# Making q, k and v of a gated attention/MLP kernel in row halves of 64 that change banks half way

## Chip, cores, metric

One Trainium2 chip; the kernel runs on 1 of its cores. The metric is the device time of one execution in microseconds. Five engines work beside each other, each through its own queue in order: TensorE (PE; its weight loads are listed apart as PEld), VectorE (DVE), ScalarE (ACT), GpSimd (POOL) and SyncE (SP), which issues the DMAs here.

## What is computed

```python
S, D, H, F = 2048, 576, 32, 4608          # Dh = 18, all float32
g = sigmoid((x * gate_w).sum(-1, keepdims=True))
q, k, v = split(x @ wqkv)                  # 3 x 32 heads of 18
a = softmax(q @ k.T * Dh ** -0.5) @ v      # per head
a = a.reshape(S, D) @ wo
y = layernorm(x)
b = gelu(y @ w1 + b1) @ w2 + b2
out = g * a + (1 - g) * b
```

## The kernel before

The work is recorded in the order in which the Python code emits it: there is no scheduler, each engine runs its instructions as written, and waits are put between them where a tile is written or read.

**Products.** Every float32 operand is split in a rounded high part and the rest (`hi`, `lo`), and a product is the sum of three: hi·hi, hi·lo, lo·hi. D = 576 is four chunks of 128 and one of 64. The last chunk's high and low part lie in one tile of 128 rows (`big[0:64, 8]`, `big[64:128, 8]`), with the weights of that chunk twice below each other. So an accumulation is 4 x 3 + 2 = 14 matmuls of 128 rows.

**The first stage** (L712 to L1022, some 216 us) makes q, k and v. x is worked on in four blocks (`tb`) of 512 tokens. Per block there are 17 groups in a list `work`: nine `qk_group` (128 output columns of wqkv, all 512 tokens: 14 matmuls of 512 columns into one PSUM bank) and eight `v_group` (128 tokens, half of v's 576 columns: 14 matmuls of 288 columns). A qk group is then copied out by ACT (`hh`, L896), its rest is made by DVE (`hl`, L897), and both go to DRAM (`qk_scr`). A v group is copied by ACT (first half, L918 and L920) or DVE (second half, L922).

After each group g the loop emits what hangs on it, "the hook of g" below:
- `x_chunk(tb + 1, c)`, in five consecutive hooks: chunk c of the next block of x is transposed by PE (four 128x128 transposes into a bank, L766). DVE subtracts the mean for the MLP (L781), ACT rounds the high part (L783), DVE makes the low part (L784); in the trace ACT starts when L781 has ended. In block 0 `y_chunk` does the like for the block's own normed rows.
- `norm`, `stat_rows`, `load_wide`: the layer norm's statistics on DVE, their transpose, and a broadcast load of mean and 1/std that L781 needs.
- `next_round`, twice in the hooks that the table `ROUNDS` names: a round of the attention's first pass, two matmuls of 54 rows (rows 0 to 53 and 64 to 117, L229) into two banks, each reduced to its maximum by DVE (L231). Forty rounds in twenty hooks lie in this stage: three hooks of block 1, nine of block 2, eight of block 3.
- loads of q, k and weights, and pieces of the MLP's preparation.

**Banks.** The stage uses eight PSUM banks: four (`ps_a`) go round among groups and transposes, and four (`ps_s1` with three, `ps_o` with one; `score_bank` goes round them) that belong to the rounds.

**After it** follow attention and MLP together: a step of scores, exponentials and P·V with pieces of the MLP between. Matmuls there are pairs of 64 rows (or 54, 56): one on rows 0 to 63 and one on rows 64 to 127, into two banks. `out_pair` (L548) exchanges them half way: in its first half (`turn` 0) rows 0 to 63 add to bank 0 and rows 64 to 127 to bank 1, in its second the other way round, so that both banks get the whole sum. So that no bank gets both at once, PE waits between the turns on a semaphore `swap` (L567), which ACT raises (`sem_inc`, L585) when both last matmuls of the first turn have ended.

## Time and profile before

| what | us |
|---|---|
| median of 3 runs | 2225.52 (2225.38 to 2226.88) |
| profiled execution, first to last instruction | 2224.1 |
| first stage: PE's last v matmul ends, first score matmul starts | 216.3 |
| its block 0, q and k; then v | to 40.1; to 60.7 |
| its blocks 1, 2, 3 | to 110.35, 165.36, 216.27 |
| ACT, POOL busy in the whole span | 1428.9, 1003.0 |

The span and the median differ by 1.4 us, which lie around the program. Times of the stage's parts are starts of instructions in the timeline. A row of the timeline merges instructions of one line: start, time from the first start to the last end, engine, line, operation, shapes (rows*columns of the weights, then output), count. As a matmul's end overlaps the next one's start, the pitch of a stream is read from starts, not from durations. The granted TensorE clock is 1.000 throughout.

### The profile page before, as it was taken

What the parts mean: (1) busy time and instruction counts of PE and PEld (TensorE: products, weight loads), DVE (VectorE), ACT (ScalarE), POOL (GpSimd) and SP (SyncE); (2) the same over time, 40 slices, a digit from 0 to 9 for tenths busy, and PEclk for the clock granted to TensorE, in tenths of its full rate; (3) what the DMA queues carried; (4) which work ended last, traced back from release to release, by engine and by line L of the source; (5) the groups of instructions that cost most, each with busy time, mean ns of one, the idle gap of its engine ahead of it and who ended that gap; (6) DMA issues with size and microseconds to landing.
All of it is one profiled execution on the core that took longest, in us unless ns stands there. A gap on an engine that the chain in (4) does not pass through costs nothing.

```text
span 2224.1 us, 51508 instructions
## 1 busy us (share of the span) xinstructions
PE 2206.3 (99%) x20528; PEld 1576.1 (71%) x20528; DVE 1642.5 (74%) x2856; ACT 1428.9 (64%) x2655; POOL 1003.0 (45%) x1001
## 2 busy tenths in 40 slices
PE   8999999999999999999999999999999999999999
PEld 7878666766667766777766776776776776776668
DVE  6685777777778778777777777777777777777734
ACT  4333777777776666666666666666665666666772
POOL 4331766666664444444444444444444444444710
PEclk9999999999999999999999999999999999999999
DMA  8767555444464623333354424232464323242264
GB/s 266 268 222 223 192 174 162 147 159 148 153 197 136 195 101 121 123 120 104 114 171 149 137 79 137 100 124 100 120 178 146 107 102 123 101 150 92 89 223 168
DMA packets 164119, 329.23 MB, mean 148 GB/s; under 512 B 56830, under 2 KB 84090, under 8 KB 153150
## 3 DMA queue, kind: packets, MB, share of 16 engines
q1 hardware_dynamic: 161782, 322.19, 44.7%
q8 instruction: 162, 2.65, 0.5%
q10 hardware_dynamic: 1968, 3.70, 0.5%
q14 instruction: 79, 0.65, 0.1%
q0 software_dynamic: 128, 0.03, 0.0%
HBM read 233.47 MB, written 96.17 MB: 148 GB/s over the span
## 4 chain that ended last, share of the span: by engine, by line
PE 91%; DVE 3%; DMA 2%; ACT 2%; issue 1%; POOL 1%; SPq 0%; DVEq 0%; ACTq 0%; POOLq 0%
PE ps L288 20%; PE ps L578 20%; PE ps L490 20%; PE ps L270 13%; PE ps L229 11%; PE ps L890 3%; PE ps L1225 3%; PE ps L911 1%; DVE m L231 1%; DMA p<-in_A_wqkv_dram 1%; ACT zz L543 1%; DMA x<-in_B_w_dram 1%; POOL w L182 0%; PE ps L766 0%; ACT p L273 0%
## 5 line engine op out<-in xcount | busy, mean ns | idle before, releaser
L231 DVE TENSOR_REDUCE m<-ps 128x1 f32<-128x512 f32 x2048 | 1311.8, 685 | 408.9 <-PE ps L229 397.6
L273 ACT ACTIVATE p<-ps 128x512 f32<-128x512 f32 x1048 | 566.8, 596 | 264.4 <-PE ps L270 260.8
L273 ACT ACTIVATE ring<-ps 128x512 f32<-128x512 f32 x1000 | 542.3, 596 | 291.6 <-PE ps L270 288.9
L490 PE MATMUL ps<-big,w 64*128 64x512 f32 x3708 | 567.1, 392 | 0.2 <-issue 0.2
L182 POOL TENSOR_SCALAR zz<-zz 128x512 f32<-128x512 f32 x288 | 178.3, 619 | 744.4 <-ACT zz L543 712.1
L578 PE MATMUL ps<-w,hh 64*128 64x288 f32 x4352 | 484.0, 294 | 1.0 <-DVE x L595 0.9
L270 PE MATMUL ps<-qa,ka 56*128 56x512 f32 x2048 | 457.1, 420 | 3.2 <-ACT p L273 1.7
L578 PEld LDWEIGHTS ps<-w,hh 64*128 64x128 f32 x4352 | 423.0, 186 | 28.8 <-DVE x L595 3.6
L229 PE MATMUL ps<-ka,qa 54*128 54x512 f32 x2048 | 433.1, 398 | 0.6
L490 PEld LDWEIGHTS ps<-big,w 64*128 64x128 f32 x3708 | 365.8, 186 | 71.4 <-issue 0.5
L182 POOL TENSOR_TENSOR zz<-zz,z 128x512 f32<-128x512 f32 x288 | 371.5, 1290 | 24.0
L270 PEld LDWEIGHTS ps<-qa,ka 56*128 56x128 f32 x2048 | 210.5, 184 | 210.6 <-DVE m L231 165.0
L578 PE MATMUL ps<-w,hl 64*128 64x288 f32 x2176 | 347.4, 292 | 0.8 <-POOL hl L182 0.8
L288 PE MATMUL ps<-p,vt 128*32 128x512 f32 x1968 | 239.2, 598 | 0.0
L229 PEld LDWEIGHTS ps<-ka,qa 54*128 54x128 f32 x2048 | 217.1, 184 | 25.3 <-DVE m L231 5.2
L578 PEld LDWEIGHTS ps<-w,hl 64*128 64x128 f32 x2176 | 230.1, 185 | 1.2 <-POOL hl L182 1.1
L288 PE MATMUL ps<-ring,vt 128*32 128x512 f32 x1872 | 227.6, 598 | 0.0
L182 POOL TENSOR_TENSOR hl<-zz,hh 128x512 fp32r<-128x512 f32 x136 | 175.1, 1287 | 11.3
L182 POOL TENSOR_TENSOR w<-x,w 128x576 fp32r<-128x576 f32 (+1 forms) x54 | 99.5, 1858 | 167.4 <-ACT w L394 141.2
L288 PEld LDWEIGHTS ps<-p,vt 128*32 128x32 f32 x1968 | 52.5, 109 | 112.1 <-issue 102.7
L288 PEld LDWEIGHTS ps<-ring,vt 128*32 128x32 f32 x1872 | 49.9, 109 | 106.5 <-issue 106.5
L595 DVE SCALAR_TENSOR_TENSOR x<-ps,x 128x288 f32<-128x288 f32 x256 | 104.1, 449 | 8.7 <-PE ps L578 8.4
(123 smaller groups left out, 1549.8 us busy)
## 6 DMA issues: line engine op xcount, KB each, us to landing
w<-w_scr SPq DMA_DIRECT2D x54, 1152.0 KB
w<-w_scr SPq DMA_DIRECT2D x108, 576.0 KB
x<-in_B_w_dram SPq DMA_DIRECT2D x72, 288.0 KB
w_scr<-w SPq DMA_DIRECT2D x18, 1152.0 KB
w_scr<-w SPq DMA_DIRECT2D x36, 576.0 KB
qa<-qk_scr SPq DMA_DIRECT2D x192, 72.0 KB
ka<-qk_scr SPq DMA_DIRECT2D x84, 144.0 KB
qk_scr<-hh SPq DMA_DIRECT2D x36, 256.0 KB
```

Of the source, the lines that this page charges most:

```text
L182: fn(*args, **kw)
L229: nc.tensor.matmul(ps, qa[r0:r0 + 54, t * P:(t + 1) * P], ka[r0:r0 + 54, kb * TB:(kb + 1) * TB], start=True, stop=True)
L231: nc.vector.tensor_reduce(M4[u][:, h, t, kb:kb + 1], ps, axis=AX.X, op=ALU.max)
L270: nc.tensor.matmul(ps[h], ka[r0:r0 + 56, kc * P:(kc + 1) * P], qa[r0:r0 + 56, qb * TB:(qb + 1) * TB], start=True, stop=True)
L273: nc.scalar.activation(p_of(n)[:, qb, h], ps[h], AF.Exp, scale=SCALE)
L288: nc.tensor.matmul(OB[u][r:r + 32, :], v[:, k, 19 * h:19 * h + 32], p_of(c)[:, qb, h, :], start=(k == 0), stop=(k == NT - 1))
L490: nc.tensor.matmul(ps[h], wt[w_][r, c, :], y[r, c, :], start=(k == 0), stop=(k == 26))
L543: defer(2, lambda w=w, z=z: nc.scalar.activation(w, z, AF.Square))
L578: mm = nc.tensor.matmul(ps[nn][:, :ND], h_[r, tok], w_[p_][r, cs[nn]], start=(k == 0), stop=(k == 6 * G - 1))
L595: nc.vector.scalar_tensor_tensor(dst, ps[nn][:, :ND], 0.5, b2b[:, cs[nn]] if g == 0 else dst, op0=ALU.mult, op1=ALU.add)
L890: nc.tensor.matmul(ps, w_[:, c, ms], big[:, s_, :], start=(k == 0), stop=False)
L1225: nc.tensor.matmul(ps[:, :ND], OT[b][2][:, s_, tok], w_part(w_, c)[:, cs], start=(k == 0), stop=(k == 13))
```

## The change

From block 0's v on there are no groups. A *unit* (`half_unit`) makes two output tiles at once, in two banks of `ps_a`: two qk tiles, both halves of v for 128 tokens, or the tile 4 alone in two halves of 256 tokens. It runs as pairs of 64-row matmuls in two turns, 14 pairs and 13, with the exchange of banks and the `swap` semaphore between. Units go two by two through the stage: first turn of A, first turn of B, second turn of A, second turn of B. Blocks are not kept apart: v's last unit of a block goes with q/k's first of the next. Hooks stand after each turn (after the second only, for tile 4), again 17 a block, and their tables are moved by one place here and there.

Transposes become pairs of 64 rows, into two banks of `score_bank` rather than one of `ps_a`; what reads them works on 256 columns, twice. The last chunk's missing row halves are kept in `X4`, which lies in K's second buffer `KA[1]`; two rows of ones are copied back there at step 5 of the attention. Block 0's q and k, with the transposes before them, stay as they were.

```diff
-        def transposed(tb, c):
-            ps = psum(ps_a)
-            for t in range(4):
-                nc.tensor.transpose(ps[:, t * P:(t + 1) * P], x_view(tb)[:, t, c * P:(c + 1) * P], ident)
-            return ps
+        def turned_over(src, rows=P):
+            banks = [score_bank() for _ in range(2)]
+            for t, part in enumerate(src):
+                for h in range(2):
+                    r = slice(64 * h, 64 * h + 64)
+                    nc.tensor.transpose(banks[h][:rows, 64 * t:64 * t + 64], part[r], ident[r, r])
+            return banks
...
             if tb > 0:
-                nc.vector.tensor_tensor(y, ps, wide[:, 0, :], op=ALU.subtract)
+                for ps, of in pieces:
+                    nc.vector.tensor_tensor(of(y), ps, of(wide[:, 0, :]), op=ALU.subtract)
             if c < 4:
-                nc.scalar.activation(big[:, c, :], ps, AF.Copy)
-                nc.vector.tensor_tensor(big[:, 4 + c, :], ps, big[:, c, :].bitcast(F32), op=ALU.subtract)
+                for ps, of in pieces:
+                    nc.scalar.activation(of(big[:, c, :]), ps, AF.Copy)
+                    nc.vector.tensor_tensor(of(big[:, 4 + c, :]), ps, of(big[:, c, :]).bitcast(F32), op=ALU.subtract)
...
+        def half_unit(unit, turn):
+            kind, tb, a, b = unit["of"]
+            if turn == 0:
+                unit["ps"] = [psum(ps_a) for _ in range(2)]
             else:
+                nc.tensor.wait_ge(swap, unit["turned"])
+            ps = unit["ps"]
+            terms = [(c, k) for c in range(4) for k in range(3)] + ([(4, 1)] if turn else [(4, 0), (4, 2)])
+            for i, (c, k) in enumerate(terms):
+                ends = []
+                for h in range(2):
+                    o = h ^ turn
+                    r = slice(64 * h, 64 * h + 64)
+                    w_ = (W_V if kind == "v" else W_QK)[k // 2][r, c, :]
+                    xs = x_rows(tb, k % 2, c, h)
...
+                    ends.append(nc.tensor.matmul(out_, left, right, start=(turn == 0 and i == 0), stop=(turn == 1 and i == 12)))
+            if turn == 0:
+                unit["turned"] = exchange(ends)
+                return
...
+        units = [("v", 0, t, None) for t in range(4)]
+        for tb in range(1, NB):
+            units += [("qk", tb, 4, None)] + [("qk", tb, fst, snd) for fst, snd in ((0, 1), (2, 3), (5, 6), (7, 8))]
+            units += [("v", tb, t, None) for t in range(4)]
...
+        for i in range(0, len(units), 2):
+            for half in range(2):
+                for unit_ in units[i:i + 2]:
+                    kind, tb, _, snd = unit_["of"]
+                    half_unit(unit_, half)
+                    if kind == "v" or snd is not None or half == 1:
...
+                        hooked(tb, nth[tb])
+                        nth[tb] += 1
```

`exchange` is the `sem_inc` of `out_pair` as a function: one ACT instruction that waits for both matmuls in `ends`.

PE in block 2, from the end of a qk group or turn over the hook that holds a chunk of x and two rounds (hook 7; `ps` is a bank, `big` x's transposed parts, `wqk` weights, `ka_108` the `X4` parts). Before:

```order
L892 MATMUL ps<-big,wqk_126 128x512
L893 MATMUL ps<-big,wqk_127 128x512
L766 MATMUL ps<-ident,x 128x128 [waits DVE_49]
L766 MATMUL ps<-ident,x 128x128 x3
L229 MATMUL ps<-ka_107,qa_104 128x512 [waits DVE_49] x4
L890 MATMUL ps<-big,wqk_126 128x512 [waits DVE_49]
```

The same place in the change:

```order
L956 MATMUL ps<-ka_108,wqk_126 128x512
L956 MATMUL ps<-big,wqk_126 128x512
L773 MATMUL ps<-ident,x 128x64 [waits DVE_49] x2
L773 MATMUL ps<-ident,x 128x64 x6
L229 MATMUL ps<-ka_107,qa_104 128x512 [waits DVE_49,PE_49] x4
L956 MATMUL ps<-big,wqk_126 128x512 [waits swap]
```

All six instructions work in halves of 64 rows now, and the rounds' four matmuls (L229) wait for banks that the chunks of x have just used: the transposes and the rounds go round the same four.

DVE at the same place, hooks 6 to 9 of block 2 (`hl` are q/k's low parts, `p` and `big` what is made of a chunk of x, `m` the maxima of the rounds). Before:

```order
L897 TENSOR_TENSOR hl<-ps,hh 128x512
L781 TENSOR_TENSOR p<-ps,qa_106 128x512
L784 TENSOR_TENSOR big<-ps,big 128x512
L897 TENSOR_TENSOR hl<-ps,hh 128x512
L781 TENSOR_TENSOR p<-ps,qa_106 128x512
L784 TENSOR_TENSOR big<-ps,big 128x512
L231 TENSOR_REDUCE m_1041<-ps 128x1 x4
```

In the change:

```order
L801 TENSOR_TENSOR p<-ps,qa_106 128x4x64 x2
L805 TENSOR_TENSOR big<-ps,big 128x4x64 x2
L970 TENSOR_TENSOR hl<-ps,hh 128x512 x2
L801 TENSOR_TENSOR p<-ps,qa_106 128x4x64 x2
L805 TENSOR_TENSOR big<-ps,big 128x4x64 x2
L231 TENSOR_REDUCE m_1405<-ps 128x1 x4
```

The low parts of a unit come two at a time, ahead of the hook's chunk, and the chunk's own work is in pieces of 256 columns.

PE at the start of block 0's v (`wv_128` and `wv_129` are the high and low parts of v's weights). Before:

```order
L892 MATMUL ps<-big,wqk_126 128x512
L893 MATMUL ps<-big,wqk_127 128x512
L911 MATMUL ps<-wv_128,big 128x288 [waits DVE_49,Activation_49]
L911 MATMUL ps<-wv_129,big 128x288 [waits Pool_49]
L911 MATMUL ps<-wv_128,big 128x288 x2
```

In the change:

```order
L914 MATMUL ps<-big,wqk_127 128x512
L956 MATMUL ps<-wv_128,big 128x288 [waits DVE_49,Activation_49] x2
L956 MATMUL ps<-wv_128,big 128x288 x2
L956 MATMUL ps<-wv_129,big 128x288 [waits Pool_49]
L956 MATMUL ps<-wv_129,big 128x288 [waits DVE_49]
```

The third pair needs the low weights of both halves of v, the first made by POOL and the second by DVE; before, the second half's were first read 14 matmuls later.

## Prediction

> **What bounds the kernel now.** First the page: span, busy times, the chain that ended last.

> ```profile
> span 2224.1 us, 51508 instructions
> ...
> PE 2206.3 (99%) x20528; PEld 1576.1 (71%) x20528; DVE 1642.5 (74%) x2856; ACT 1428.9 (64%) x2655; POOL 1003.0 (45%) x1001
> ...
> PE 91%; DVE 3%; DMA 2%; ACT 2%; issue 1%; POOL 1%; SPq 0%; DVEq 0%; ACTq 0%; POOLq 0%
> ```

> PE is busy for 99% and is 91% of the chain, so what PE saves in the first stage moves the end, unless another engine then holds it. Attention keeps its order. Next, the stage in windows (block 0's v, blocks 1, 2, 3; columns PE, PEld, DVE, ACT, POOL):

> ```profile
> 40.00:61.00 21.00, 20.25 (x155) 19.59 (x154) 16.13 (x28) 7.63 (x18) 6.42 (x5) 1.00 0.71 238
> 61.00:110.00 49.00, 48.27 (x269) 41.60 (x269) 32.48 (x69) 14.86 (x33) 13.48 (x11) 1.00 0.81 269
> 110.00:165.00 55.00, 54.89 (x299) 43.82 (x295) 44.24 (x89) 19.78 (x39) 18.55 (x15) 1.00 0.65 225
> 165.00:216.00 51.00, 51.00 (x275) 40.71 (x273) 30.80 (x56) 16.60 (x28) 11.04 (x6) 1.00 0.70 224
> ```

> PE is full in all four. DVE comes next: 44.2 of 55 us in block 2, 16.1 of 21 in block 0. Whatever PE saves, DVE must keep up with.

> **Part 1: one matmul in 28 goes.** The timeline gives pitches, from start to start: full groups first, then 64-row pairs in attention.

> ```profile
> 44.56 1.76 PE L911 MATMUL ps<-wv,big 128*128 128x288 f32 x12
> ...
> 46.43 0.60 PE L766 MATMUL ps<-ident,x 128*128 128x128 f32 x4
> ...
> 67.21 2.91 PE L890 MATMUL ps<-big,wqk 128*128 128x512 f32 x12
> ...
> 70.41 2.91 PE L890 MATMUL ps<-big,wqk 128*128 128x512 f32 x12
> ...
> 698.50 0.96 PE L578 MATMUL ps<-w,w 64*128 64x288 f32 x12
> 699.29 0.41 PE L229 MATMUL ps<-ka,qa 54*128 54x512 f32 x2
> ...
> 776.24 1.10 PE L490 MATMUL ps<-big,w 64*128 64x512 f32 x8
> 777.16 0.41 PE L229 MATMUL ps<-ka,qa 54*128 54x512 f32 x2
> 777.40 1.10 PE L490 MATMUL ps<-big,w 64*128 64x512 f32 x8
> ```

> A v group takes 46.43 - 44.56 = 1.87, 0.133 a matmul of 14; a 64-row pair of 288 columns (699.29 - 698.50) / 6 = 0.132. A qk group takes 70.41 - 67.21 = 3.20, 0.229 a matmul; a pair of 512 columns (777.40 - 776.24) / 5 = 0.232. So a pair costs what a full matmul costs, and 27 pairs replace 28 matmuls. v: 16 units save 0.13 each, 2.1. q and k: 12 units fall from 6.40 to 27 x 0.232 = 6.26, 1.7 in all; tile 4's pairs have 256 columns, which no row shows: between half of 0.232 and 0.132 I take 0.118, 27 of them 3.19 against 3.20, nothing. **Saved: 3.8** (between -1 and +1 of that for tile 4).

> **Part 2: PE no longer changes between 128 and 64 rows.** Twenty hooks have rounds of 54 rows between full groups. One of them:

> ```profile
> 91.49 0.29 PE L914 MATMUL ps<-wv,big 128*128 128x288 f32 x1
> 91.71 0.74 PE L229 MATMUL ps<-ka,qa 54*128 54x512 f32 x4
> 92.38 1.85 PE L911 MATMUL ps<-wv,big 128*128 128x288 f32 x12
> 94.07 0.29 PE L913 MATMUL ps<-wv,big 128*128 128x288 f32 x1
> ```

> From 91.49 to 94.07 are 2.58 us for 13 v matmuls (13 x 0.132 = 1.72) and two pairs of 512 columns (0.46): 0.40 too much. In attention no such excess stands between 64-row and 54-row pairs: the five pairs from 776.24 run at one pitch. **Saved: 20 x 0.40 = 8.0.**

> **Part 3: transposes.** Two chunks at once, in block 0's v:

> ```profile
> 48.71 1.03 PE L766 MATMUL ps<-ident,x 128*128 128x128 f32 x8
> 49.50 1.84 PE L911 MATMUL ps<-wv,big 128*128 128x288 f32 x12
> ```

> Eight take 0.79, 0.10 each with 128 columns loaded and 128 moving. Eight half-row ones of 64 moving columns replace four. If loads set the pitch, four pairs cost the same 0.4; if moving columns do, 0.2; if the halves don't overlap, 0.8. I take 0.4, since the loads keep their 128 columns: 20 chunks, nothing gained (-4 to +8).

> [...]

> **Part 4: the waits that go, and those that come.** Before, the 176.2 us from 40.10 to 216.27 hold 27 qk groups (86.4), 32 of v (59.8 at 1.87), 20 chunks (8.0), 40 rounds (9.3), the excess (8.0) and some 0.5 of small transposes: 172.0. So PE waits **4.2** in all, and these waits I replace by new ones.

> *The start of v.* The timeline there:

> ```profile
> 40.10 1.76 PE L911 MATMUL ps<-wv,big 128*128 128x288 f32 x12
> ...
> 41.03 1.65 DVE L761 TENSOR_TENSOR wv<-p,wv 128x1440 fp32r<-128x1440 f32 x1
> ...
> 42.74 1.72 PE L911 MATMUL ps<-wv,big 128*128 128x288 f32 x11 [0.47 <-DVE wv L761]
> ```

> DVE ends the second half's low weights at 42.68. The change needs them in its third pair, at 40.36, so PE waits 2.4 until 42.74, with all of v behind it. DVE's order ahead of that instruction is unchanged. **+2.4.**

> *Banks.* Transposes and rounds share four banks now. The latencies, from timelines and from groups of the first 40 us:

> ```profile
> 63.78 0.39 PE L893 MATMUL ps<-big,wqk 128*128 128x512 f32 x1
> ...
> 64.25 0.60 ACT L896 ACTIVATE hh<-ps 128x512 fp32r<-128x512 f32 x1 [1.14 <-issue]
> ...
> 64.88 0.69 DVE L897 TENSOR_TENSOR hl<-ps,hh 128x512 fp32r<-128x512 f32 x1 [0.83 <-ACT hh L896]
> ...
> 134.51 2.48 DVE L231 TENSOR_REDUCE m<-ps 128x1 f32<-128x512 f32 x4
> ...
> L761 DVE TENSOR_TENSOR wqk<-p,wqk 128x256 fp32r<-128x256 f32 x1 | 0.4, 418 | 0.0
> L760 ACT ACTIVATE wqk<-p 128x256 fp32r<-128x256 f32 x1 | 0.4, 405 | 0.0
> ```

> Block 2, hook 7: let P be the time at which PE goes on after the turn (64.00 in these rows). ACT starts at P + 0.25, the first low part at P + 0.88. DVE's pitch is some 0.6 at 512 columns (2.48 for four) and 0.34 at 256 (0.42 less the same overlap). So the unit's two low parts take DVE to P + 2.1, and the chunk's four pieces end at P + 3.7. The hook's second round needs this chunk's two banks: PE gets there at P + 0.7 and gets them at P + 3.4 and 3.8. Wait: 3.1. Behind it in PE's queue is the whole next turn. Hook 9, by the same steps, with the rounds in both preceding chunks' banks: 2.4. Block 1, hook 10: DVE has hook 9's four reductions (2.5) ahead of the chunk, so the banks come at P + 6.6 of the turn before: 3.8. **Sum 9.3**; at the least nothing, if DVE is ahead.

> Smaller ones by the same steps: DVE's lag at the end of block 0's v 0.4, hooks 11 and 16 of block 2 1.4, five hooks of rounds in a row in block 3 1.6, ACT's pieces of the MLP ahead of v's copies at the stage's end 1.2, the last unit's banks at the MLP's first matmul 0.6: 5.2. Each hangs on a few tenths; I take half, **2.6** (0 to 5.2).

> *Semaphore.* Each exchange needs one ACT instruction:

> ```profile
> L585 ACTq EVENT_SEMAPHORE  x144: 17/17/17, 255.3 to 2134.7; - x144
> ...
>   PEld ps L578: 1.2, 6
> ```

> In attention 144 of these held PE six times, 1.2 in all. Here the other unit's turn (1.8 or 3.2) lies between. Nothing; if ACT is late, see the rivals.

> DVE's and ACT's extra pieces (256 columns twice) are in the latencies above. POOL's two memsets less and the two copies at step 5 lie beside PE's work: nothing.

> **Sum**, against the profiled span: -3.8 - 8.0 - 4.2 + 2.4 + 9.3 + 2.6 = -1.7, 2222.4; the median lies 1.4 above the span: **2224**.

> **Rivals.**
> *A, the forecast:* banks eat the gain. For it: DVE's 44.2 us in block 2, and units whose low parts come two at a time ahead of the chunk. 2224; with the smaller waits between none and all, and 3 us either way for the transposes and the large waits, 2219 to 2228.

> [...]

> *B, banks come in time:* if PE's waits shrink to the start of v and at most half of the 9.3, the sum is -13.6 to -9: 2212 to 2217. For it: before, DVE ran without a pause for long in block 2 and PE lost little. Against it: those rounds had four banks to themselves.

> *C, the semaphore, slower:* `sem_inc` stands in ACT's queue behind copies that wait for DVE. When ACT is later than the other unit's turn, 1.8 in v, PE waits at the exchange. If most of v's 16 exchanges lose 0.5 on top of A, that is 8: 2232.

> *D, no single mode:* if half-row transposes of 64 columns or the exchange cost a drain like the rounds did, 8.0 comes back: 2232.

> **How the numbers follow.** A 0.47, B 0.28, C 0.20, D 0.05. A measurement tells 0.2% from no change, 4.5 us: faster is below 2221.1. That is B and a fifth of A: 0.38. Same: the rest of A but its top, 0.36. Slower: C, D and that top, 0.26. The range leaves out B's best cases and the worse half of C and D: 2213 to 2231. A's own is 2219 to 2228.

> **What would show it.** Part 1 and 2: pitches of 0.13 and 0.23 for the unit's pairs, and no excess around L229 in the stage. Part 3: the pitch of the L773 pairs, 0.1. Part 4: PE idle 2.4 at 40.4 for v's weights; gaps of 2 to 4 us ahead of L229 in hook 10 of block 1 and hooks 7 and 9 of block 2, ended by DVE's pieces of a chunk; the stage ending at 213 to 217 instead of 216.3. Waits put down to ACT at the exchange would speak for C. The prediction is wrong if the half-row transposes cost twice, or if DVE's pieces of 256 columns are far from 0.42.

## The result, and the profile after

The changed kernel takes **2244.45 us** (median of 5, 2242.23 to 2246.21) against 2225.52 (median of 5, 2225.22 to 2226.88): ratio 1.0082, 95% interval 1.0071 to 1.0093. It is slower by 18.9 us, where 2224 was forecast with 2231 as the upper end. The profiled execution took 2242.23 us, the shortest of the five; its span is 16.3 us longer than that of before, and it is these 16.3 that the trace can explain. From the page of the changed kernel:

```profile
span 2240.4 us, 53493 instructions
...
PE 2203.1 (98%) x21459; PEld 1583.4 (71%) x21459; DVE 1647.1 (74%) x2901; ACT 1431.7 (64%) x2684; POOL 999.7 (45%) x999
...
PE 87%; DVE 3%; POOL 2%; ACT 1%; issue 1%; DMA 0%; SPq 0%; DVEq 0%; POOLq 0%; ACTq 0%
```

PE is busy for 3 us less in a span that is 16 us longer. The windows show where (changed kernel, the columns of before: PE, PEld, DVE, ACT, POOL busy, then the granted clock):

```profile
40.00:61.00 21.00, 17.65 (x277) 16.69 (x278) 15.86 (x39) 7.79 (x24) 5.94 (x5) 1.00 0.62 208
61.00:110.00 49.00, 43.46 (x449) 37.51 (x447) 30.26 (x75) 12.15 (x32) 9.92 (x8) 0.93 0.75 241
110.00:165.00 55.00, 49.03 (x535) 45.35 (x531) 41.48 (x99) 17.44 (x45) 18.21 (x15) 0.97 0.68 211
165.00:216.00 51.00, 49.38 (x525) 43.10 (x525) 31.50 (x60) 16.86 (x31) 7.55 (x6) 1.00 0.81 241
```

PE was full in all four; now it idles 3.4, 5.5, 6.0 and 1.6 us of them, and in two the clock is no longer 1.00. The view of PE's waits in the stage, before first, then after (us in total, times, longest; only named releasers):

```profile
PE ps L766 <- DVE big L784: 0.7, 1, 0.7
PE ps L911 <- DVE wv L761: 0.5, 1, 0.5
PE ps L911 <- DVE big L784: 0.3, 1, 0.3
```

```profile
PE ps L229 <- DVE big L805: 8.1, 4, 3.7
PE ps L229 <- ACT oe L246: 1.8, 1, 1.8
PE ps L956 <- DVE wv L763: 1.7, 1, 1.7
PE ps L229 <- DVE ka L811: 1.3, 2, 0.8
...
PE ps L229 <- ACT strow L857: 1.0, 1, 1.0
```

Over nine of these microseconds stand ahead of a score round (L229) and end with DVE's pieces of an x chunk (L805, L811): the banks that transposes and rounds share.

**An account of the stage**, from the first matmul of v to the first L270. *Work* is each matmul at the pitch of its kind (the pitches of the prediction; 0.09 for a pair of transposes); *waits* are the times from one start to the next above that pitch, where they exceed 0.25 us (they come out larger than the idle times of the views, because a matmul's end overlaps the next one's start: 0.39 long at a pitch of 0.23 with 512 columns); *clock* is what matmuls took longer in stretches granted 0.5; *small* is the rest, in which the mode changes of before lie (0.40 a hook of rounds in the prediction's rows). The last column goes from the first L270 to the last P·V matmul (L288 in both kernels).

| kernel | stage | work | small | waits | clock | time behind, against before |
|---|---|---|---|---|---|---|
| before | 176.2 | 163.7 | 8.4 | 4.0 | 0 | 0 |
| changed | 189.3 | 158.5 | 0.9 | 26.3 | 3.6 | +3.3 |
| e_share | 187.8 | 163.7 | 7.5 | 10.2 | 6.3 | +0.4 |
| e_full | 198.1 | 159.3 | 7.5 | 25.5 | 5.8 | +2.0 |
| e_rounds | 184.4 | 158.5 | 0.3 | 20.9 | 4.7 | +7.0 |
| e_b3 | 175.8 | 158.5 | 0.5 | 16.7 | 0 | +7.1 |
| e_c4 | 170.2 | 158.5 | 0.5 | 11.1 | 0 | +1.4 |

The gain came in full: 5.2 of work and 7.5 of mode changes. Against it stand 22.3 more of waits and 3.6 of clock: 13.1 net. The other 3.3 us are lost in attention, whose order did not change. The 7.0 and 7.1 of e_rounds and e_b3 hold the same losses, with 6.8 us at half clock behind the wait near 520 (and 3.4 more near 2141 in e_rounds); e_share loses another 0.8 behind its last P·V matmul.

### The profile page after: what moved, and what is told of

The parts are those of the page before. It is cut to its first block, busy times and chain, and to the rows that moved or that the text cites. A ratio compares the mean times of both kernels' runs of the same rounds, so it can differ in the third digit from the quotient of the medians.

```text
span 2240.4 us, 53493 instructions
## 1 busy us (share of the span) xinstructions
PE 2203.1 (98%) x21459; PEld 1583.4 (71%) x21459; DVE 1647.1 (74%) x2901; ACT 1431.7 (64%) x2684; POOL 999.7 (45%) x999
## 4 chain that ended last, share of the span: by engine, by line
PE 87%; DVE 3%; POOL 2%; ACT 1%; issue 1%; DMA 0%; SPq 0%; DVEq 0%; POOLq 0%; ACTq 0%
PE ps L288 20%; PE ps L495 20%; PE ps L583 19%; PE ps L270 12%; PE ps L229 10%; PE ps L956 3%; PE ps L1300 3%; DVE m L231 1%; POOL zz L182 1%; ACT zz L548 1%; DMA low<-ot_scr 0%; PE ps L244 0%; ACT p L273 0%; DVE x L596 0%; POOL w L182 0%
## 5 line engine op out<-in xcount | busy, mean ns | idle before, releaser
L231 DVE TENSOR_REDUCE m<-ps 128x1 f32<-128x512 f32 x2048 | 1311.8, 684 | 412.2 <-PE ps L229 398.4
L270 PE MATMUL ps<-qa,ka 56*128 56x512 f32 x2048 | 457.1, 421 | 4.4 <-ACT p L273 1.8
L229 PE MATMUL ps<-ka,qa 54*128 54x512 f32 x2048 | 439.9, 398 | 14.6 <-DVE big L805 8.1
L270 PEld LDWEIGHTS ps<-qa,ka 56*128 56x128 f32 x2048 | 210.6, 184 | 211.9 <-DVE m L231 165.3
L229 PEld LDWEIGHTS ps<-ka,qa 54*128 54x128 f32 x2048 | 222.2, 185 | 39.5 <-issue 6.9
L288 PE MATMUL ps<-p,vt 128*32 128x512 f32 x1968 | 239.2, 598 | 0.0
L288 PE MATMUL ps<-ring,vt 128*32 128x512 f32 x1872 | 227.6, 598 | 0.0
L288 PEld LDWEIGHTS ps<-p,vt 128*32 128x32 f32 x1968 | 52.6, 109 | 112.1 <-issue 102.8
L288 PEld LDWEIGHTS ps<-ring,vt 128*32 128x32 f32 x1872 | 50.0, 109 | 106.4 <-issue 106.4
```

The source lines that it names most:

```text
L229: nc.tensor.matmul(ps, qa[r0:r0 + 54, t * P:(t + 1) * P], ka[r0:r0 + 54, kb * TB:(kb + 1) * TB], start=True, stop=True)
L231: nc.vector.tensor_reduce(M4[u][:, h, t, kb:kb + 1], ps, axis=AX.X, op=ALU.max)
L270: nc.tensor.matmul(ps[h], ka[r0:r0 + 56, kc * P:(kc + 1) * P], qa[r0:r0 + 56, qb * TB:(qb + 1) * TB], start=True, stop=True)
L288: nc.tensor.matmul(OB[u][r:r + 32, :], v[:, k, 19 * h:19 * h + 32], p_of(c)[:, qb, h, :], start=(k == 0), stop=(k == NT - 1))
```

## The experiments

Times are medians, each beside runs of the kernel before on the same chip (2225.0 to 2225.5).

**One part alone, in the kernel before: e_share.**

```
-            ps = psum(ps_a)
+            ps = psum(ps_a) if first else score_bank()
```

> The kernel before, with one part of the change alone: the transposes of x behind the first block (20 chunks) go into the four score banks, which the rounds use, instead of the groups' four. No pairs, no new order, 128 rows. If the sharing of the banks by itself makes PE wait, gaps of 1 to 3 us ahead of L229 appear in block 2 at the hooks that have a chunk and rounds (7 and 9) and in block 0's v, 6 to 12 us in all: 2231 to 2239. If the waits come from the tempo instead (a PE that has become 7% faster ahead of a DVE with no less to do), the slower order before the change has room for most of them: 3 us or less, 2226 to 2229.

Measured: 2237.5, ratio 1.0050 (1.0033 to 1.0067). From its waits, timeline (start, duration, engine, line, operation; in brackets the idle time before and what ended it) and windows:

```profile
PE ps L229 <- DVE big L784: 4.2, 3, 2.4
PE ps L229 <- DVE big L789: 2.0, 1, 2.0
```

```profile
142.66 0.69 DVE L897 TENSOR_TENSOR hl<-ps,hh 128x512 fp32r<-128x512 f32 x1 [0.64 <-ACT hh L896]
143.27 0.68 DVE L781 TENSOR_TENSOR p<-ps,qa 128x512 f32<-128x512 f32 x1
...
144.62 0.69 DVE L784 TENSOR_TENSOR big<-ps,big 128x512 fp32r<-128x512 f32 x1 [0.66 <-ACT big L783]
...
145.46 0.46 PE L229 MATMUL ps<-ka,qa 54*128 54x512 f32 x1 [2.41 <-DVE big L784]
```

```profile
142.60:146.00 3.40, 0.99 (x5) 0.35 (x4) 2.67 (x5) 0.63 (x2) 1.26 (x1) 1.00 0.42 154
146.00:149.40 3.40, 3.40 (x9) 2.63 (x10) 1.70 (x3) 0.00 (x0) 0.00 (x0) 0.50 0.02 5
```

The chain is the prediction's at hook 7: group's low part, chunk's subtraction, ACT's copy, chunk's low part, and only then the round. It makes the stage 11.6 us longer without a single pair: 6.2 of waits and 6.3 of clock, less 0.9 of small excess. At hooks 7 and 9 of block 2 the waits are 4.9, against 5.2 in the changed kernel: there the shared banks alone are enough, at the old tempo as well, and the rival of the tempo falls. In the whole stage e_share has 6.2 of new waits, the changed kernel 22.3. Block 0's v, where waits had been expected too, has none here and 2.4 behind its first waits in the changed kernel: there the tempo or the pieces of 256 columns must take part, and no run separates these.

**The banks' phase in attention: e_ring and e_ringb.** Where attention's steps begin, `ring[0] += 2` in the changed kernel, `ring[0] += 3` in the kernel before.

> The changed kernel, with the counter that picks the next score bank set on by two where attention's steps begin, so that the steps find the phase modulo 5 that they had before the change (80 banks drawn until then before, 128 after). Phase theory: the +3.8 us that the changed kernel loses behind the first L288 (one step of 2.3 to 2.5 near 520 us, 1.3 near 2140) and part of the 1.2 us that its first L270 waits for v's last copy come from that phase; then the waits near 529 and 2142 vanish and the time falls by 4 to 5 us, to about 2240. Chance theory: those stalls are transfers that land at other moments; then they stay or move, and the time stays within 1.5 us of 2244.5.

> The kernel before, with the same counter set on by three where the steps begin, so that it has the changed kernel's phase and nothing else of the change. Phase theory: stalls of 2.3 to 2.5 us near 517 us and 1.3 near 2125 appear, and up to 1.2 at the first L270: 2229 to 2231. Chance theory: 2225.5, within 1 us.

Measured: 2240.13 (2239.45 to 2241.99), 4.3 below the changed kernel; and 2228.51, ratio 1.0017 (1.0008 to 1.0027), 3.5 above the kernel before. Timelines of e_ringb, and of the changed kernel at the same step:

```profile
515.83 0.50 PE L270 MATMUL ps<-qa,ka 56*128 56x512 f32 x1 [0.67 <-DVE m L231]
...
518.29 0.79 PE L229 MATMUL ps<-ka,qa 54*128 54x512 f32 x1 [1.49 <-DVE m L231]
```

```profile
529.40 0.50 PE L270 MATMUL ps<-qa,ka 56*128 56x512 f32 x1 [0.67 <-DVE m L231]
...
531.86 0.50 PE L229 MATMUL ps<-ka,qa 54*128 54x512 f32 x1 [1.49 <-DVE m L231]
```

The same two waits, to the hundredth, come with the phase, and in e_ring's trace this step has neither. Which bank a step draws depends on how many were drawn before it, and the change draws 128 where 80 were drawn. In e_ringb the two were followed by 6.8 us at half clock, so the same step costs 2.5 us in the changed kernel's trace and 5.4 in this one. Why just this phase lets an L270 meet a bank that DVE still reads stays open.

The wait near 2140, which the same expectations put down to the phase, does not belong to it: 1.3 us in the changed kernel, it is still 1.1 in e_ring and 1.2 in e_c4, both with the phase of before, and e_ringb, with the changed one, has next to none (0.2). In the changed kernel PE waits there for DVE, and DVE for a load:

```profile
2141.38 0.69 DVE L1213 TENSOR_TENSOR x<-x,low 128x512 f32<-128x512 f32 x1 [7.84 <-DMA low<-ot_scr]
...
2142.49 0.77 PE L583 MATMUL ps<-w,hh 64*128 64x288 f32 x3 [1.36 <-DVE x L596]
```

Every run with the new stage has this wait (0.6 to 2.9), e_share does not; why the load comes later against PE's work is open. So of the 3.3 us lost in attention the phase is 2.5 and this wait 1.3; 0.6 is gained near 416.

**Rounds away from the chunks: e_rounds.** Only the two rows of the table of rounds change:

```
-lambda g: 2 * (g in (9, 10, 16)), lambda g: 2 * (g % 2 or g == 16),
+lambda g: 2 * (g in (9, 15, 16)), lambda g: 2 * (g in (2, 4, 5) or g > 10),
```

> The changed kernel with the score rounds moved off the hooks that transpose x: block 1 hooks 9, 15, 16 instead of 9, 10, 16; block 2 hooks 2, 4, 5 and 11 to 16 instead of 1, 3, 5, 7, 9, 11, 13, 15, 16. The same 40 rounds. Theory of the shared banks: the waits of 4.0 (block 1, hook 10), 3.05 and 2.2 (block 2, hooks 7 and 9) and 1.3 (hook 3) go, some tenths come at the new places; PE's busy share stays over half in every 3.4 us, so the granted clock stays 1.0 there and another 3 to 4 us come back: the stage ends 10 to 13 us earlier, 216 to 219 instead of 229.35, and the time is 2231 to 2235. Rival, DVE is behind anyway: the waits only move to the next users of the banks, and the stage ends at 226 or later.

Measured: 2238.58, stage end 224.87. It lies between the two: the named waits went, and of their 10.6 us half came back at the new places:

```profile
110.45 0.46 PE L229 MATMUL ps<-ka,qa 54*128 54x512 f32 x1 [0.81 <-DVE ka L811]
...
111.77 0.47 PE L229 MATMUL ps<-ka,qa 54*128 54x512 f32 x1 [0.86 <-DVE ka L811]
```

```profile
133.99 2.48 DVE L231 TENSOR_REDUCE m<-ps 128x1 f32<-128x512 f32 x4
...
134.74 2.29 PE L229 MATMUL ps<-ka,qa 54*128 54x512 f32 x4 [0.46 <-DVE m L231]
```

DVE has 2.5 us of reductions for a hook of two rounds and up to 1.5 more of low parts or sums, in a turn of 1.85 or 3.2: where the rounds stand close, it is late again.

**Rounds to where DVE has room: e_b3.** The same 40 rounds, most of them in block 3, one a hook in v's turns.

```
+lambda g: 2 * (g in (9, 16)), lambda g: {2: 1, 5: 1, 12: 1, 13: 1, 14: 1, 15: 1, 16: 2}.get(g, 0),
+lambda g: 2 if g < 10 or g == 16 else 1]
```

> The changed kernel with most score rounds moved into block 3, where DVE has room, one a hook in the stretches of v: block 1 hooks 9 and 16 (two each), block 2 hooks 2, 5 and 12 to 15 (one each) and 16 (two), block 3 two in each of the first ten hooks and in the last, one in the others. The same 40 rounds. Theory that PE waits because DVE has more to do in a turn than the turn is long, and holds the shared banks meanwhile: with one round or none in a turn that has a chunk, the waits in blocks 1 and 2 fall from 17 us to 5 or less and block 3 gets 1 to 3: the stage ends at 214 to 219, 2229 to 2235. Rival, the banks' count alone decides (two banks for a chunk, two for a round, whatever DVE does): waits stay near 20, and the stage ends at 225 or later.

Measured: 2231.79, stage end 216.06, no stretch at half clock in the stage. The waits in blocks 1 and 2 fell from 15 to 6. So the banks' count alone is not the bound: with two banks for a chunk and two for a round most of PE's waits there go, if DVE can empty them within the turn. In the whole stage 16.7 are left.

**PE kept busy: e_warm.** Pairs of no use between the two rounds of block 1's hook 10 (16) and block 2's hook 9 (10); what they write is written over.

> The changed kernel with matmuls of no use put between the two rounds of block 1's hook 10 (16 pairs of 64 rows and 512 columns, 3.7 us) and of block 2's hook 9 (10 pairs, 2.3 us), into banks that the next unit starts afresh, so that PE works through two of the waits. Clock theory: the wait at hook 10 makes PE idle for over half of two windows of 3.4 us, and the two windows behind run at half clock; kept busy, PE keeps 1.0, no stretch at 0.5 stays in the stage, and the 3.6 us that its matmuls lost there come back, less what the useless work overruns the waits (0.5 or so): 2240 to 2242. Rival, the clock falls for another reason, or costs nothing because DVE is late anyway: stretches of 0.5 stay, or the stage ends no earlier than 229.

Measured: 2241.43 (2239.41 to 2246.6), the profiled one 2246.6, with the stage's end at 233.31. Inconclusive: the median lies in the forecast range, but stretches at 0.5 stayed, as its rival had it. Behind the smaller waits ahead of hook 10 a stretch at 0.5 began at 99.1 already, and further ones came at 150, 167 and 222, so the cost of the clock was not isolated in this way.

**Full transposes again: e_full.**

```
-            if first:
-                ps = psum(ps_a)
+            if True:
+                ps = psum(ps_a) if first else score_bank()
```

> The changed kernel with one part undone: behind the first block, the transposes of x are again four of 128 rows into one score bank for each chunk (20 chunks), and their readers work on 512 columns at once. Theory that full rows between 64-row pairs cost a mode switch as the rounds did before the change: each chunk shows 0.2 to 0.4 us above its transposes, 4 to 8 us in all, against which one bank for each chunk instead of two and DVE pieces of 0.69 instead of twice 0.42 take 5 to 10 us from the waits of 26.3: the stage ends at 223 to 231 and the time is 2238 to 2246. Rival, the switch costs nothing with transposes and only the fuller banks count: the stage ends at 220 or earlier.

Measured: 2249.05, ratio 1.0107 (1.0092 to 1.0122). Small excess rose from 0.9 to 7.5, 0.33 for each of 20 chunks, as the mode theory has it; but the waits stayed, so the single bank for a chunk brought nothing, and that part of the expectation was wrong. In this stream of pairs half-row transposes were the right ones.

**Small things, and both together: e_small, e_best2.**

```
-6: (2, (0, 1)), 7: (3, (2,)), 8: (3, (3,))}
+7: (2, (0, 1)), 8: (3, (2, 3))}
...
-            if tb == 1 and g == 5:
+            if tb == 1 and g == 4:
                 load_q(0)
...
+                nc.vector.tensor_copy(mr, ps[:32, :P])
...
+    ring[0] += 2
```

> The changed kernel with five small things moved, each at a place of its own: the first block's last two norm steps behind the split of v's second half of weights; load_q and load_k of block 1 at hook 4 instead of 5, ahead of the store of the statistics; in block 0 x's chunk ahead of y's in each hook; the copy of the maxima's transposed rows by DVE instead of ACT in the stage; and the phase of e_ring. Theory by places: v's first waits fall from 2.8 to about 1; the wait at block 1's hook 10 falls from 4.0 to about 1.7, since the broadcast of the statistics lands 2.4 us earlier; the wait of 1.07 at block 1's first unit goes; the wait of 2.06 that ends on ACT's copy goes; the waits behind the stage as in e_ring. In all 7 to 9 us of stage with 2 of clock, and the time about 2231. Rival: DVE's backlog holds PE anyway, and half or more of it comes back at the next banks: 2236 or more.

> The changed kernel with the edits of e_small and e_b3 together. If both theories hold, the waits of 26.3 us in the stage fall to 7 to 10, no stretch runs at half clock, the stage ends at 204 to 210, and the time is 2212 to 2218: faster than both kernels. If DVE's backlog is the bound, the stage ends at 214 or later, and the time is 2222 or more.

Measured: 2238.79 and 2228.03. Two of the edits did what was said: the wait on L246 is gone, and hook 10's wait fell from 4.0 to 1.55. V's first waits fell from 2.8 to 1.9 only, where about 1 was said, and the edit of the phase took away the wait near 520, but not that near 2140. In the changed kernel hook 10's wait had hung on a transfer:

```profile
88.11 3.17 SPq L138 DMA_DIRECT2D ka<-qk_scr  x6
...
93.28 0.58 SPq L858 DMA_DIRECT2D st_scr<-strow  x1
...
96.77 0.32 SPq L862 DMA_DIRECT2D qa<-st_scr  x1
...
101.08 0.76 DVE L801 TENSOR_TENSOR p<-ps,qa 128x256 f32<-128x256 f32 x2 [2.40 <-DMA qa<-st_scr]
...
102.52 1.10 PE L229 MATMUL ps<-ka,qa 54*128 54x512 f32 x2 [3.66 <-DVE big L805]
```

```profile
99.83 0.75 DVE L804 TENSOR_TENSOR p<-ps,qa 128x256 f32<-128x256 f32 x2
...
101.27 1.09 PE L229 MATMUL ps<-ka,qa 54*128 54x512 f32 x2 [1.17 <-DVE big L808]
```

The statistics' rows were ready (ACT, 86.8 to 87.1), but their store stood in SP's queue behind the loads of q and k and went at 93.28; DVE then waited 2.40 for the broadcast. In e_small (second fence) it doesn't wait. The fourth edit, x's chunk ahead of y's in block 0, made a new wait of 2.5 and one of 1.3 at 62 to 63 and a stretch at half clock behind them, in both kernels. With it e_small's stage gained 1.4 instead of 7 to 9 (its clock term is 8.6), and e_best2 missed its 2212 to 2218.

**Without that edit: e_best3, e_c4, e_best4.** e_best3 leaves it out and has no round in the hook of the maxima's transpose. e_c4 adds this, for x's chunk 4, where ACT and DVE took turns:

```
-                    for hi, lo, r in ((X4[64:128, tb, :], big[64:128, 8, :], slice(64, 128)),
-                                      (big[0:64, 8, :], X4[0:64, tb, :], slice(0, 64))):
-                        nc.scalar.activation(of(hi), ps[r], AF.Copy)
-                        nc.vector.tensor_tensor(of(lo), ps[r], of(hi).bitcast(F32), op=ALU.subtract)
+                    nc.scalar.activation(of(X4[64:128, tb, :]), ps[64:128], AF.Copy)
+                    nc.scalar.activation(of(big[0:64, 8, :]), ps[0:64], AF.Copy)
+                for ps, of in pieces:
+                    nc.vector.tensor_tensor(of(big[64:128, 8, :]), ps[64:128], ...
+                    nc.vector.tensor_tensor(of(X4[0:64, tb, :]), ps[0:64], ...
```

e_best4 moves four of y's chunks, and the load of block 2's x, into block 1.

> The edits of e_best2 without the one that put x's chunk ahead of y's in block 0 (its profile had new waits of 2.5 and 1.3 us at 61.7 and 63.0 and a stretch of 6.8 us at half clock behind them), and with no score round in the hook of block 3 that transposes the maxima's rows. Theory of DVE's backlog: those waits fall back to some 3 us spread over block 0's v, the wait of 1.9 ahead of that transpose goes, nothing runs at half clock: the stage ends at 211 to 214 and attention takes 1 us more than before: 2221 to 2224. Rival, the gain is used up elsewhere: the stage ends at 216 or later, 2226 or more.

> e_best3, and in chunk 4 of x the four copies of ACT stand ahead of the four subtractions of DVE, where they took turns. The chain of ACT and DVE there takes 3.4 us in e_best2 (147.7 to 151.2) and PE waits behind it at 64 to 65, 112 and 151, 2.8 us in all. If the taking of turns is what makes it long, it falls to 2.7 or less and 1 to 2 us of those waits go: 2219 to 2223. Rival: the copies, now all ahead, hold the banks as long, and nothing changes beside e_best3.

> e_c4, and four of y's five chunks of block 0 moved from the hooks of v, where DVE has 2.7 us of work in a turn of 1.85, into block 1's first two hooks, where it is free for a third of the time; x of block 2 is loaded there instead of at block 0's last hook, and the statistics start a hook later. Theory of DVE's backlog: the waits of 3 us at 53 to 65 fall to under 1, at most one comes back in block 1: 2217 to 2221. Rival: the load of x comes too late for block 2's statistics and the broadcast, and the wait at 97 to 103 grows by as much.

Measured: 2224.17 (ratio 0.9993, 0.9984 to 1.0002), **2221.97 (0.9985, 0.9976 to 0.9993)**, and 2229.38 (1.0015). e_c4 beats both kernels, by 3.2 and 22.5 us; its stage ends 6.2 earlier than before's, and its waits are 2.6 below those of e_best3. Some 1.7 of these stand behind chunk 4, whose chain of ACT and DVE in block 2 fell from 3.0 to 2.5, so the taking of turns had made it slow; 0.6 stand at the start of v, which this edit does not touch. In e_best4 block 2's x came late: its statistics' transpose made PE wait 5.1 us at 89.4 for DVE, the rival's case.

## Why the prediction was wrong

**Part 1, right:** 3.8 said, 4.4 by the account (work of the units, 146.1 to 141.7). Thirteen pairs of 512 columns lie between 186.71 and 189.69, 0.229 each:

```profile
186.71 3.14 PE L956 MATMUL ps<-big,wqk 64*128 64x512 f32 x26
...
189.69 0.39 PE L956 MATMUL ps<-big,wqk 64*128 64x512 f32 x1
```

**Part 2, right:** 8.0 said, 7.5 by the account. Two pairs of rounds between pairs of q, k and v take 0.47, with nothing on top:

```profile
93.54 0.85 PE L229 MATMUL ps<-ka,qa 54*128 54x512 f32 x4
94.01 1.84 PE L956 MATMUL ps<-wv,big 64*128 64x288 f32 x23
```

**Part 3, right in kind:** nothing said, 0.8 gained at the account's 0.09 a pair. Here eight pairs take 0.60, 0.075 each instead of 0.1; what sets this pitch, loads or moving columns, no run shows:

```profile
50.49 0.72 PE L773 MATMUL ps<-ident,x 64*128 64x64 f32 x15
...
51.09 1.92 PE L956 MATMUL ps<-wv,big 64*128 64x288 f32 x24
```

**Part 4 failed, in the size of its terms.** The old waits went (4.2 said, 4.0). Of the new ones, the start of v cost 2.8 for 2.4. "Banks" had 9.3 for three hooks: hook 7 of block 2 took 3.05 for 3.1, hook 9 took 2.2 for 2.4, but block 1's hook 10 took 6.1 for 3.8 (4.0 ahead of its second round, the rest just before), since the working let DVE start the chunk behind its reductions and left out the broadcast that it needs, for which DVE waited 2.40. Hook 7, where the working held:

```profile
146.98 1.29 DVE L970 TENSOR_TENSOR hl<-ps,hh 128x512 fp32r<-128x512 f32 x2 [0.67 <-ACT hh L969]
...
148.18 0.75 DVE L801 TENSOR_TENSOR p<-ps,qa 128x256 f32<-128x256 f32 x2
...
149.05 0.76 DVE L805 TENSOR_TENSOR big<-ps,big 128x256 fp32r<-128x256 f32 x2
...
149.62 0.80 PE L229 MATMUL ps<-ka,qa 54*128 54x512 f32 x2 [2.70 <-DVE big L805]
```

The step that failed worst is "Smaller ones": half of 5.2 was taken, and 12.1 came. Block 0's v took 2.4 for 0.4 (DVE has 2.3 us of chunk work and v's copies in turns of 1.85); block 2's hook 11 1.9; the maxima's transpose 0.6 and the round that waits for ACT's copy of it 2.1, where ACT was thought to hold v's copies; the statistics' rows at block 2's hook 3 1.3, and others, not seen at all. Taking half of a list of waits was the wrong turn: most of them end with DVE, whose lateness goes on from one turn to the next, so they came together. That they did so for this one reason is our reading; e_b3 and e_c4, where DVE has room and 26.3 falls to 16.7 and 11.1, speak for it.

**Two terms were missing.** The clock: 3.6 in the stage. The time in attention: 3.3, which the forecast had at nothing because "Attention keeps its order". Its order was kept, its banks were not (2.5), and a load came later against PE's work (1.3, cause open).

In sum the waits were 12.0 too low, clock and attention, 6.9, were missing, and the terms of the gain were off by some 0.8 in the other direction: within rounding the 18.0 from -1.7 to the 16.3 measured on the spans. Neither of the two signs of being wrong that the prediction named came (the pair of transposes takes 0.075, DVE's two pieces 0.76); the end of the stage showed it, 229.3 where 213 to 217 was said.

**The rivals.** B fell; e_c4, with the rounds where DVE has room, comes nearer to it, but still waits 11.1 and lies above its 2212 to 2217. C did not happen: nothing in the stage waits for the instruction of the exchange. D did not happen. A's mechanism was right, and its price stopped at what the large hooks cost. In the changed kernel's trace, but for 1.9 for v's weights, nearly all of the 26.3 us end with DVE or ACT reading a bank (16.5 of the 18.7 that the view of PE's waits lists with a releaser).

## What to carry to other kernels

When work moves into banks that another stream uses, count for every turn what the engine that empties them must do within it, against the turn's new, shorter length (in block 0's v DVE had 2.3 us of a chunk's work, and v's copies, for a turn of 1.85); here that was more than the turn, and the smaller waits came to 12.1 us, not to a few tenths. Follow the producers of what that engine reads as well, through the DMA queue (DVE waited 2.40 for a broadcast here). A count that sets a rotation (banks drawn so far) is part of the state that a change hands to unchanged code: look at what the unchanged part waits for as well (2.5 us here).

## What the runs showed of the hardware

```profile
97.00:100.30 3.30, 1.45 (x9) 0.69 (x9) 1.68 (x4) 0.00 (x0) 0.00 (x0) 1.00 0.73 199
100.30:107.10 6.80, 4.58 (x39) 4.56 (x41) 3.90 (x8) 0.71 (x2) 1.27 (x1) 0.50 0.80 226
...
154.90:158.30 3.40, 1.69 (x19) 1.15 (x17) 3.16 (x9) 2.06 (x5) 2.14 (x2) 1.00 1.02 308
158.30:161.80 3.50, 3.49 (x26) 3.43 (x28) 2.58 (x5) 0.00 (x0) 1.59 (x2) 0.51 0.71 231
```

Waits of 1.15 and 1.1 in one step (154.9 to 158.3, PE busy for 1.69 of 3.40) were enough for the next to be granted 0.51.

In e_share twelve matmuls of 512 columns took 4.46 (111.15 to 115.61) over one step at half clock, and 2.75 (63.16 to 65.91) at full clock: 1.71 more, half of 3.41. So a wait of some 2 us can cost up to 1.7 more for each step at half clock, an estimate from these rows; the changed kernel's three steps cost 3.6 in all. The length of a wait alone did not decide: the wait of 3.05 at hook 7 brought no stretch in the changed kernel and 6.8 us of them in e_small; in e_share a wait of 2.41 at this hook was followed by 3.4. The five runs of the changed kernel, 4 us apart, go with their mean clock: 2242.2 and 2242.3 at 0.998, 2244.5 twice at 0.996, 2246.2 at 0.995. That the place on the grid makes the difference is our reading. No experiment took the clock's part away by itself.
